# One quarter of a weight load, issued as sixteen pieces of eight partitions

## The chip, the cores and the metric

One core of a Trainium2 chip runs the kernel. The metric is the device time of one execution in microseconds (us); the time before is the median of three runs. The profile is one execution more, recorded by the hardware profiler, and it has its own time. The core's compute engines are PE (matrix multiply, its results go to PSUM), DVE (elementwise and reductions), ACT (activation functions) and POOL. SP (SyncE) computes nothing: it issues the transfers, in program order, and 16 DMA engines carry them between HBM and SBUF, the on-chip memory of 128 partitions.

## The reference, cut to what matters

Four requests decode one token each: attention of 32 heads over a cache of 4096 keys and values, an output projection `wo`, then a dense block with a mish activation. Weights and caches are bfloat16.

```python
x = A_x                                                   # [4, 1, 640]
q = (layernorm(x) @ wq) as [b, h, 1, 128]
scores = einsum("bhqd,bhkd->bhqk", q, k_cache) * 128**-0.5    # k_cache [4, 32, 4096, 128]
o = einsum("bhqk,bhkd->bhqd", softmax(scores), v_cache)
h = x + o as [4, 1, 4096] @ wo                            # wo [4096, 640]
hh = layernorm(h) @ w1 + b1                               # w1 [640, 1728]
out = h + (hh * tanh(softplus(hh))) @ w2                  # w2 [1728, 640]
```

K and V are 134 MB each; all weights together are 15 MB.

## The kernel before

The work goes in 32 steps g (`NG`), each with four heads of one request: g = 4 * hq + b, hq a group of four heads, b the request. One step needs one K tile and one V tile, each [128 partitions, 128 rows, 128], 32 KB a partition and 4.19 MB in all. A partition holds 128 keys of one head, so a tile is one transfer with 128 long contiguous rows (`load_kv`, issue on L91). Both pools have two buffers (`KBUFS`, `VBUFS`); only the last K and V tiles come in two halves.

In step g, DVE multiplies the K tile by the broadcast query (L297), PE adds up the products with identity matmuls in PSUM (L304), DVE finishes the sums (L316), and PE, DVE and ACT make the softmax one step later (L329 to L347). PE multiplies the V tile of step g-1 by the softmax weights (`pv`, L231).

The order of the issues on SP is written out by hand in the loop: after the products of step g comes the K load of step g+2 (L374), then `pv(g - 1)`, then the V load of step g+1 (L383). The K load waits until the K buffer is free, that is until DVE and PE are done with K of step g; the V load waits until PE is done with V of step g-1.

`wo` (4096 x 640, 5.24 MB) comes into the buffer that `wq` used, `wo_sb`, in four quarters of `WOC` = 8 heads, at steps 8 to 11 (`WO_AT`), each right behind that step's V load. A quarter is one transfer: `(h p) n -> p h n` puts row h*128+p into partition p, so each partition gets eight runs of 640 elements, 1280 bytes each, 1024 runs in all. Behind the first quarter goes `b1` as a single row. Its first readers: `project(hq)` (L274) multiplies four heads of `wo_sb` with the normalised attention; groups 0 to 3 run at steps 14 to 17, group 6 at step 30 and group 7 after the loop (`PROJ_AT`), and the last quarter holds the heads of groups 6 and 7.

The dense block's weights follow behind the last V tile: w1 in one transfer into a freed K buffer (L421), w2 in five (L422 to L425).

A framework adds the semaphores from the program's reads and writes. Each DMA signals on one of eight completion semaphores, which it takes in turn over all DMAs of the program (`DMAHW0` to `DMAHW7` in the built program). A DMA that takes a semaphore is held, on SP, until the transfer that had it before has landed, unless SP has seen that already.

Of the kernel before, what the change touches and what calls it, by code (L numbers as in the profile page):

```python
# [16 lines left out]
def kernel(  # L17
# [21 lines left out]
    nc = tc.nc  # L39

    B, Sq, D = A_x.shape
    _, H, Sk, Dh = A_k_cache.shape
# [14 lines left out]
    WOC = 8  # L57
# [36 lines left out]
    def load_k(g):  # L94
        return load_kv(kpool, "kt", A_k_cache, g)

    def load_v(g):
        return load_kv(vpool, "vt", A_v_cache, g)
# [35 lines left out]
    for q in range(G):  # L134
        nc.vector.tensor_copy(
            out=sel[:, :, q, q * PH : (q + 1) * PH],
            in_=ident[0:N, 0:N].unsqueeze(2).to_broadcast([N, N, PH]),
# [45 lines left out]
    def q_chunk(n):  # L183
        q_ps = ps.tile([N, QC], FP32, tag="qq")
        for c in range(DC):
            nc.tensor.matmul(  # L186
                q_ps[:, :],
                lhsT=xT[:, c, :],
                rhs=wq_sb[:, c, n * QC : (n + 1) * QC],
                start=(c == 0),  # L190
                stop=(c == DC - 1),
            )
        nc.scalar.copy(out=q_all[:, n * QC : (n + 1) * QC], in_=q_ps[:, :])  # L193
# [31 lines left out]
    def pv(g):  # L225
        hq, b = divmod(g, N)
        vt = vts.pop(g)
        if b == 0:
            ot[hq] = ps.tile([128, N, G], FP32, tag="ot", bufs=2, name=f"ot{hq}")
        for r in range(R):  # L230
            nc.tensor.matmul(  # L231
                ot[hq][:, b, :],
                lhsT=vt[:, r, :],
                rhs=e2[g % NE2][:, r, :],
                start=(r == 0),
                stop=(r == R - 1),
            )
# [3 lines left out]
    def row_sums(hq):  # L241
        l_ps = ps.tile([128, N, G], FP32, tag="small")
        nc.tensor.matmul(  # L243
            l_ps[:, :, :],
            lhsT=ones_f[:, :],
            rhs=rs2[:, hq * N : (hq + 1) * N, :],
            start=True,
            stop=True,
        )
        rls[hq] = work.tile([128, N, G], FP32, tag="rl", name=f"rl{hq}")  # L250
        nc.vector.reciprocal(out=rls[hq][:, :, :], in_=l_ps[:, :, :])  # L251

    def normalise(hq):
        nc.vector.tensor_tensor(
            out=otn[:, hq, :, :],
            in0=ot.pop(hq)[:, :, :],
            in1=rls.pop(hq)[:, :, :],
            op=ALU.mult,
        )
# [12 lines left out]
    wo_sb = []  # L272

    def project(hq):  # L274

        for h in range(hq * G, (hq + 1) * G):
            for c in range(DC):
                nc.tensor.matmul(  # L278
                    yT[:, c, :],
                    lhsT=wo_sb[0][:, h, c * 128 : (c + 1) * 128],  # L280
                    rhs=otn[:, hq, :, h % G],
                    start=(h == 0 and c == 0),
                    stop=(h == H - 1 and c == DC - 1),
                )
# [3 lines left out]
    def mul_and_sum(g, part):  # L288

        hq, b = divmod(g, N)  # L290
        r0 = part * RP
        kt = kts[g][:, r0 : r0 + RP, :]
        s_ps = ps.tile([128, RP, W], FP32, tag="s", bufs=2, name=f"s{g}_{part}")
        s_of[g, part] = s_ps
        for k in range(NQ):
            d0 = k * DQ
            nc.vector.tensor_tensor(  # L297
                out=kt[:, :, d0 : d0 + DQ],
                in0=kt[:, :, d0 : d0 + DQ],
                in1=qbs[:, hq, b, d0 : d0 + DQ].unsqueeze(1).to_broadcast([128, RP, DQ]),  # L300
                op=ALU.mult,
            )
            for d in range(d0, d0 + DQ, W):
                nc.tensor.matmul(  # L304
                    s_ps[:, :, :],
                    lhsT=ident[:, :],
                    rhs=kt[:, :, d : d + W],
                    start=(d == 0),
                    stop=(d == Dh - W),
                )  # L310
            yield

    def finish_sum(g, part):
        if part == 0:
            s_sbs[g] = work.tile([128, R], FP32, tag="s_sb", name=f"s_sb{g}")
        nc.vector.tensor_reduce(  # L316
            out=s_sbs[g][:, part * RP : (part + 1) * RP],
            in_=s_of.pop((g, part))[:, :, :],
            axis=AX.X,
            op=ALU.add,  # L320
        )

    def softmax(g):

        s_sb = s_sbs.pop(g)
        pm = work.tile([128, 1], FP32, tag="pm", name=f"pm{g}")
        nc.vector.tensor_reduce(out=pm[:, :], in_=s_sb[:, :], axis=AX.X, op=ALU.max)  # L327
        tr_ps = ps.tile([128, 128 + G], FP32, tag="tr", name=f"tr{g}")
        nc.tensor.matmul(  # L329
            tr_ps[0:1, 0:128], lhsT=pm[:, :], rhs=ident_f[:, :], start=True, stop=True  # L330
        )
        yield
        mx = work.tile([1, G], FP32, tag="mx", name=f"mx{g}")
        nc.vector.tensor_reduce(  # L334
            out=mx[:, :],
            in_=tr_ps[0:1, 0:128].rearrange("o (a b) -> o a b", a=G),
            axis=AX.X,
            op=ALU.max,
        )

        nb_ps = tr_ps[:, 128 : 128 + G]
        nc.tensor.matmul(nb_ps, lhsT=nscale[:, :], rhs=mx[:, :], start=True, stop=True)  # L342
        nb = work.tile([128, G], FP32, tag="nbs", name=f"nbs{g}")
        nc.scalar.copy(out=nb[:, :], in_=nb_ps)  # L344
        for q in range(G):
            p0, p1 = q * PH, (q + 1) * PH
            nc.scalar.activation(  # L347
                out=e2[g % NE2][p0:p1, :, q],
                in_=s_sb[p0:p1, :],
                func=ACT.Exp,  # L350
                bias=nb[p0:p1, q : q + 1],
                scale=SCALE,
                accum_out=rs2[p0:p1, g, q : q + 1],
            )
        yield

    for g in range(NG):
        hq, b = divmod(g, N)
        for part in range(NP):
            now = mul_and_sum(g, part)  # L360
            before = None
            next(now)
            if part > 0:
                finish_sum(g, part - 1)
            elif g >= 1:
                finish_sum(g - 1, NP - 1)
                before = softmax(g - 1)
                next(before)
            next(now)
            if before is not None:  # L370
                next(before)
        kts.pop(g)
        if g + 2 < NG:
            kts[g + 2] = load_k(g + 2)  # L374
        if 1 <= g < NG - 1:
            pv(g - 1)
            if b == 0:
                row_sums(hq - 1)
                normalise(hq - 1)
        if g in PROJ_AT:  # L380
            project(PROJ_AT[g])
        if g + 1 < NG:
            vts[g + 1] = load_v(g + 1)  # L383
        for n in Q_AT.get(g, ()):
            q_chunk(n)
            q_broadcast(n)
        if g in WO_AT:

            if not wo_sb:
                wo_sb.append(wbig.tile([128, H, D], BF16, tag="w", name="wo_sb"))  # L390
            h0 = WO_AT[g] * WOC
            nc.sync.dma_start(
                out=wo_sb[0][:, h0 : h0 + WOC, :],
                in_=A_wo.rearrange("(h p) n -> p h n", p=128)[:, h0 : h0 + WOC, :],
            )
            if WO_AT[g] == 0:
                nc.sync.dma_start(out=b1_row[:, :], in_=B_b1.rearrange("(o f) -> o f", o=1))
        if g == B1_AT:
            b_ps = ps.tile([128, FC], FP32, tag="small", name="b_ps")
            for c in range(FC):  # L400
                cols, fw = f_chunk(b1_row[:, :], c)
                nc.tensor.matmul(
                    b_ps[0:fw, c : c + 1],
                    lhsT=cols,
                    rhs=ident[0:1, 0:1],
                    start=True,
                    stop=True,
                )
            nc.vector.tensor_copy(out=b1T[:, 0:C2], in_=b_ps[:, 0:C2])
            nc.vector.tensor_copy(out=b1T[0:FREM, C2:FC], in_=b_ps[0:FREM, C2:FC])  # L410
# [44 lines left out]
    for dst in (h2T, hc):  # L455
        nc.vector.tensor_tensor(
            out=dst[:, :, :],
# [11 lines left out]
    for c in range(FC):  # L469
# [9 lines left out]
        if c == 4:  # L479
# [3 lines left out]
                out=std[:, :], in_=v_ps[:, :], func=ACT.Sqrt, bias=eps_t[:, :], scale=1.0  # L483
# [5 lines left out]
        out=h1n[:, :, :],  # L489
# [6 lines left out]
        out=h1s[:, :, :],  # L496
# [9 lines left out]
        out=tb[:, :, :],  # L506
# [8 lines left out]
        out=ta[:, :, :], in0=tb[:, :, :], scalar1=-0.5, scalar2=-1.0, op0=ALU.mult, op1=ALU.add  # L515
# [4 lines left out]
        out=act_t[:, :, :],  # L520
# [10 lines left out]
    for i, (w2, c) in enumerate(w2_of):  # L531
# [11 lines left out]
        out=oT[:, :, :].rearrange("p n c -> p c n"),  # L543
# [46 lines left out]
```

## Time and profile before

| | |
|---|---|
| median of 3 runs | 678.72 us (678.62 to 679.22) |
| the profiled execution | 679.1 us, span from first to last instruction 677.2 us |
| busy PE, DVE, ACT | 467.1, 352.9, 95.1 us |
| read from HBM | 283.35 MB, 418 GB/s over the span |
| chain that ended last, K loads / w loads | 61% / 4% of the span |
| the four `wo` issues | 1280 KB each, 30.7 us (median) from issue to landing |
| K and V issues | 31 + 31 of 4096 KB, 2 + 2 of 2048 KB |

How to read it: a row of the profile names the line, the engine and the tiles (out<-in); `xcount` is how many instructions it stands for. SPq rows are issues: their duration is how long SP was held by the issue, not how long the transfer took. The slices are 40 equal parts of the span; a digit is the busy share in tenths. The chain follows the work that ended last back to what released it at each step.

### The profile page before, as it was taken

The page shows a single profiled execution, that of the slowest core. Times are in us where ns is not written, and L with a number is a line of the kernel's source. Part 1 is how long each engine was busy: PE and PEld are TensorE (multiplying, and loading weights), DVE is VectorE, ACT ScalarE, POOL GpSimd, SP SyncE. Part 2 cuts the span into 40 slices and gives each one's busy share as a digit, 9 for nine tenths or more (in the row PEclk, how much of TensorE's full clock was granted, in tenths as well). Part 3 has the DMA queues.
Part 4 walks back from the last instruction along what each step waited for, and adds up shares of the span by engine and source line. Part 5 has one row for each costly group of instructions (what it writes and reads, how often), then busy time and mean ns, then how long its engine had stood idle before and what let it go on. Part 6 is the DMA issues. An engine that isn't in the chain of part 4 may idle for free.

```text
span 677.2 us, 12413 instructions
## 1 busy us (share of the span) xinstructions
PE 467.1 (69%) x5761; PEld 258.3 (38%) x5761; DVE 352.9 (52%) x304; ACT 95.1 (14%) x313; POOL 2.4 (0%) x13
## 2 busy tenths in 40 slices
PE   1588898787676475467677668767666776666965
PEld 0234445444333341343344434323333432333444
DVE  2476445456655356336654545665454566645722
ACT  0022112212101111011100111110011111101131
POOL 1000000000000000000000000000000000000000
PEclk9997678987667786687676788876788876767875
DMA  9999999999999999999999999999999999999993
GB/s 376 434 433 429 433 430 432 432 431 430 430 431 416 429 417 411 429 423 429 433 431 428 426 431 431 429 429 433 432 429 431 429 433 433 429 426 425 431 407 144
DMA packets 15211, 284.15 MB, mean 420 GB/s; under 512 B 1267, under 2 KB 5559, under 8 KB 6584
## 3 DMA queue, kind: packets, MB, share of 16 engines
q1 hardware_dynamic: 15152, 283.36, 98.2%
q8 instruction: 45, 0.74, 0.4%
q14 instruction: 6, 0.05, 0.0%
q10 hardware_dynamic: 8, 0.01, 0.0%
HBM read 283.35 MB, written 0.01 MB: 418 GB/s over the span
## 4 chain that ended last, share of the span: by engine, by line
DMA 66%; PE 16%; DVE 16%; issue 1%; ACT 0%; SPq 0%; DVEq 0%
DMA kt<-in_A_k_cache_dram 61%; PE s L304 14%; DVE kt L297 14%; DMA w<-in_B_w_dram 4%; DVE s_sb L316 2%; PE tr L329 1%; DVE mx L334 0%; PE h_ps L472 0%; PE y2T L534 0%; PE ot L231 0%; PE q_ps L186 0%; PE qb_ps L200 0%; ACT q_all L193 0%; DVE tb L517 0%; PE var_ps L449 0%
## 5 line engine op out<-in xcount | busy, mean ns | idle before, releaser
L304 PE MATMUL s<-kt,ident 128*128 128x512 bf16 x1024 | 299.5, 446 | 175.0 <-DVE kt L297 174.8
L297 DVE TENSOR_TENSOR kt<-kt,qbs 128x4096 bf16<-128x4096 bf16 x128 | 291.5, 2279 | 219.0 <-DMA kt<-in_A_k_cache_dram 219.0
L304 PEld LDWEIGHTS <-ident 128*128 128x128 bf16 x1024 | 107.8, 109 | 326.3 <-issue 178.4
L231 PEld LDWEIGHTS <-vt 128*128 128x128 bf16 x4096 | 109.0, 96 | 11.3 <-DMA vt<-in_A_v_cache_dram 2.2
L231 PE MATMUL ot<-e,vt 128*128 128x4 bf16 x4096 | 109.0, 165 | 4.0 <-DMA vt<-in_A_v_cache_dram 2.1
L347 ACT ACTIVATE e<-s_sb,nbs 32x128 bf16<-32x128 f32 x128 | 74.0, 578 | 2.5
L344 ACT COPY nbs<-tr 128x4 f32<-128x4 f32 x32 | 5.2, 162 | 467.3 <-PE tr L342 467.3
L316 DVE TENSOR_REDUCE s_sb<-s 128x64 f32<-128x512 f32 x64 | 43.5, 680 | 3.6 <-PE s L304 3.6
L347 ACT ACTIVATION_READ_ACCUMULATOR e<-s_sb,nbs 32x1 f32 x128 | 32.2, 252 | 0.0
L251 DVE RECIPROCAL rl<-l_ps 128x16 f32<-128x16 f32 x8 | 2.1, 257 | 45.3 <-PE l_ps L243 45.3
L334 DVE TENSOR_REDUCE mx<-tr 1x4 f32<-1x128 f32 x32 | 8.9, 279 | 30.5 <-PE tr L329 30.5
L186 PE MATMUL q_ps<-wq_sb,xT 128*4 128x512 bf16 x40 | 14.7, 517 | 9.2 <-DMA wq_sb<-in_A_wq_dram 9.2
L200 PE MATMUL qb_ps<-q_all,sel 4*128 4x128 bf16 x128 | 13.6, 286 | 5.3 <-ACT q_all L193 5.3
L329 PE MATMUL tr<-ident_f,pm 128*1 128x128 f32 x64 | 16.0, 344 | 1.2 <-DVE pm L327 1.2
L200 PEld LDWEIGHTS <-sel 4*128 4x128 bf16 x128 | 12.3, 128 | 10.7 <-issue 10.7
L193 ACT CAST q_all<-q_ps 4x512 bf16<-4x512 f32 x8 | 4.6, 574 | 74.6 <-PE q_ps L186 74.6
L342 PEld LDWEIGHTS tr<-mx,nscale 1*128 1x128 f32 x64 | 9.4, 183 | 13.8 <-issue 11.5
L329 PEld LDWEIGHTS tr<-ident_f,pm 128*1 128x1 f32 x64 | 2.8, 81 | 26.0 <-issue 26.0
L342 PE MATMUL tr<-mx,nscale 1*128 1x4 f32 x64 | 12.2, 258 | 0.4 <-DVE mx L334 0.4
L327 DVE TENSOR_REDUCE pm<-s_sb 128x1 f32<-128x128 f32 x32 | 9.2, 286 | 1.1
L186 PEld LDWEIGHTS <-xT 128*4 128x4 bf16 x40 | 3.4, 97 | 15.1 <-issue 13.5
L278 PE MATMUL yT<-otn,wo_sb 128*128 128x4 bf16 x160 | 5.5, 165 | 1.9 <-issue 1.6
(74 smaller groups left out, 51.1 us busy)
## 6 DMA issues: line engine op xcount, KB each, us to landing
kt<-in_A_k_cache_dram SPq DMA_DIRECT2D x31, 4096.0 KB, 25.7
vt<-in_A_v_cache_dram SPq DMA_DIRECT2D x31, 4096.0 KB, 32.0
wq_sb<-in_A_wq_dram SPq DMA_DIRECT2D x1, 5120.0 KB, 14.9
wo_sb<-in_A_wo_dram SPq DMA_DIRECT2D x4, 1280.0 KB, 30.7
kt<-in_A_k_cache_dram SPq DMA_DIRECT2D x2, 2048.0 KB, 23.1
vt<-in_A_v_cache_dram SPq DMA_DIRECT2D x2, 2048.0 KB
w<-in_B_w_dram SPq DMA_DIRECT2D x1, 2160.0 KB, 28.4
w<-in_B_w_dram SPq DMA_DIRECT2D x3, 640.0 KB, 19.9
```

The source lines that it names most:

```text
L186: nc.tensor.matmul(q_ps[:, :], lhsT=xT[:, c, :], rhs=wq_sb[:, c, n * QC : (n + 1) * QC], start=(c == 0), stop=(c == DC - 1),)
L200: nc.tensor.matmul(qb_ps[:, b * Dh : (b + 1) * Dh], lhsT=sel[:, b, q, :], rhs=q_all[:, h * Dh : (h + 1) * Dh], start=(q == 0), stop=(q == ...
L231: nc.tensor.matmul(ot[hq][:, b, :], lhsT=vt[:, r, :], rhs=e2[g % NE2][:, r, :], start=(r == 0), stop=(r == R - 1),)
L278: nc.tensor.matmul(yT[:, c, :], lhsT=wo_sb[0][:, h, c * 128 : (c + 1) * 128], rhs=otn[:, hq, :, h % G], start=(h == 0 and c == 0), stop=(h ...
L297: nc.vector.tensor_tensor(out=kt[:, :, d0 : d0 + DQ], in0=kt[:, :, d0 : d0 + DQ], in1=qbs[:, hq, b, d0 : d0 + DQ].unsqueeze(1).to_broadcas ...
L304: nc.tensor.matmul(s_ps[:, :, :], lhsT=ident[:, :], rhs=kt[:, :, d : d + W], start=(d == 0), stop=(d == Dh - W),)
L316: nc.vector.tensor_reduce(out=s_sbs[g][:, part * RP : (part + 1) * RP], in_=s_of.pop((g, part))[:, :, :], axis=AX.X, op=ALU.add,)
L327: nc.vector.tensor_reduce(out=pm[:, :], in_=s_sb[:, :], axis=AX.X, op=ALU.max)
L329: nc.tensor.matmul(tr_ps[0:1, 0:128], lhsT=pm[:, :], rhs=ident_f[:, :], start=True, stop=True)
L334: nc.vector.tensor_reduce(out=mx[:, :], in_=tr_ps[0:1, 0:128].rearrange("o (a b) -> o a b", a=G), axis=AX.X, op=ALU.max,)
L342: nc.tensor.matmul(nb_ps, lhsT=nscale[:, :], rhs=mx[:, :], start=True, stop=True)
L347: nc.scalar.activation(out=e2[g % NE2][p0:p1, :, q], in_=s_sb[p0:p1, :], func=ACT.Exp, bias=nb[p0:p1, q : q + 1], scale=SCALE, accum_out=r ...
```

## The change

The issue of a `wo` quarter becomes a loop over the partitions. For the first three quarters it runs once, over all 128. For the last quarter (`h0 + WOC == H`, step 11) it runs sixteen times, over eight partitions each; a piece is 8 partitions x 8 runs of 1280 bytes, 80 KB. The sixteen pieces write what the one transfer wrote, on the same queue and at the same place in the program: behind V of step 12, ahead of K of step 14.

```diff
@@ -389,10 +389,15 @@
             h0 = WO_AT[g] * WOC
-            nc.sync.dma_start(
-                out=wo_sb[0][:, h0 : h0 + WOC, :],
-                in_=A_wo.rearrange("(h p) n -> p h n", p=128)[:, h0 : h0 + WOC, :],
-            )
+
+            pp = 8 if h0 + WOC == H else 128
+            for p0 in range(0, 128, pp):
+                nc.sync.dma_start(
+                    out=wo_sb[0][p0 : p0 + pp, h0 : h0 + WOC, :],
+                    in_=A_wo.rearrange("(h p) n -> p h n", p=128)[
+                        p0 : p0 + pp, h0 : h0 + WOC, :
+                    ],
+                )
             if WO_AT[g] == 0:
```

The pieces take sixteen turns of the eight completion semaphores where the one transfer took one. Every DMA behind them takes another of the eight than before.

## The prediction

> **What bounds the kernel now.** I read the page first: the DMA rows of the slices, the queues, the chain.
>
> ```profile
> DMA  9999999999999999999999999999999999999993
> GB/s 376 434 433 429 433 430 432 432 431 430 430 431 416 429 417 411 429 423 429 433 431 428 426 431 431 429 429 433 432 429 431 429 433 433 429 426 425 431 407 144
> ...
> q8 instruction: 45, 0.74, 0.4%
> ...
> q10 hardware_dynamic: 8, 0.01, 0.0%
> ...
> DMA 66%; PE 16%; DVE 16%; issue 1%; ACT 0%; SPq 0%; DVEq 0%
> ...
> x_bf<-in_A_x_dram ACTq DMA_DIRECT2D x1, 5.0 KB
> ```
>
> The 16 DMA engines are full in 39 of 40 slices at about 432 GB/s, 27 GB/s each. DVE and PE sit on the chain only between two K loads. So time is what the engines must carry, plus any stretch in which they have nothing queued. The q10 row is for later: a load of 4 rows left 8 packets, four with data and four that close it.
>
> Second, the end of the run by windows (last two columns: share of the 16 engines, GB/s).
>
> ```profile
> 656.00:662.00 6.00, 3.67 (x118) 3.58 (x118) 0.26 (x1) 0.00 (x0) 0.00 (x0) 0.50 0.99 379
> 662.00:668.00 6.00, 3.45 (x81) 3.19 (x79) 1.20 (x8) 0.00 (x0) 0.00 (x0) 0.50 0.56 218
> 668.00:672.00 4.00, 1.90 (x51) 1.90 (x51) 1.74 (x7) 2.00 (x4) 0.00 (x0) 0.50 0.29 118
> ```
>
> The share falls to about half at 662 us and the rest runs on to 671: half of the engines are done nine microseconds early. The packet records say which: the 45 instruction fetches (q8, 16 KB) go round eight engines only, and each puts its engine back by 1.6 us. I call these the later eight, the others the earlier eight. At vt12 (the V load of step 12) the earlier eight close at 287.4 to 288.7 us, the later eight at 290.6 to 292.4.
>
> Third, SyncE's own line of time around the last quarter of wo (start, duration).
>
> ```profile
> 249.53 11.22 SPq L91 DMA_DIRECT2D kt<-in_A_k_cache_dram  x1
> 260.86 4.90 SPq L91 DMA_DIRECT2D vt<-in_A_v_cache_dram  x1
> 265.81 0.43 SPq L392 DMA_DIRECT2D wo_sb<-in_A_wo_dram  x1
> 272.67 11.27 SPq L91 DMA_DIRECT2D kt<-in_A_k_cache_dram  x1
> 284.04 6.12 SPq L91 DMA_DIRECT2D vt<-in_A_v_cache_dram  x1
> ```
>
> These are kt13, vt12, the last quarter, kt14 and vt13. kt14 is handed over at 272.67 and lands 33.6 us later, at 306.2: it stands more than 20 us deep in the queue, which is why the engines never run dry.
>
> Fourth, the chain in order of time (start, length).
>
> ```profile
> 249.53 33.56 DMA kt<-in_A_k_cache_dram
> ```
> ```profile
> 638.29 28.37 DMA w<-in_B_w_dram
> ```
>
> kt13 lands at 283.1. The end hangs on w1, which the later eight bring at 666.7; a delay of the later eight in the middle thus reaches the end whole.
>
> **The change, part by part.** *Computation.* No compute instruction is added or moved, and the bytes are the same. The quarter is first read by the projection of step 30, some 300 us later, so its own landing may slip at no cost.
>
> *Who carries the bytes.* A store of 20 rows at the end shows how a short transfer is spread:
>
> ```profile
> DMA packets 30, 0.01 MB, mean 2 GB/s; under 512 B 30, under 2 KB 30, under 8 KB 30
> ...
> out_dram<-out_bf SPq DMA_DIRECT2D x1, 5.0 KB
> ```
>
> 30 packets are 20 rows and 10 closings, so ten engines of two rows; the 4-row load used four. Eight rows then go to eight engines, one each. Followed packet by packet, b1's single row and two of the four rows of x sit on engines of the earlier eight, so I put the pieces there. [...] Today each engine carries 64 packets of 1280 B; vt11 lands at 268.7 and the third quarter behind it at 272.3 (242.88 + 29.4), so a quarter takes 3.5 us. After the change the earlier eight carry 128 packets, 7.1 us, and the later eight none: -3.5 us on the eight that set the end.
>
> *SyncE's waits.* This is where I see the cost. In the built program each DMA takes one of eight completion semaphores in turn and waits until the last transfer on that semaphore has landed. One wo DMA used up one turn; sixteen go round twice. Pieces 0 to 3 go at once (265.8 to 267.5). Piece 4 waits for vt11 (268.7), piece 5 for the third quarter (272.3), piece 6 for kt13 (283.1), piece 7 for vt12. vt12 has no landing row; the quarter behind it landed at 265.81 + 30.7 = 296.5, less 3.5 gives 293.0. kt14 and vt13 stand behind these on SyncE, and kt13 and vt12 were the last large loads in the queue. So the cover of 20 us is used up, and the later eight go idle when vt12 is through.
>
> *Restart.* From 293.0 SyncE issues pieces 7 to 15 and then kt14. An issue cost 0.33 us (plain K load) to 0.58 (the first V load); I take the wo row, 0.43, since it is the same kind: 9 x 0.43 = 3.9, so kt14 goes at 296.9 (295.9 to 298.2). Piece 15 waits for piece 7, kt14 for piece 8; both have long landed. From issue to first data the store of the result took 0.8 us; wq, on empty queues, landed 14.9 us after its issue, where 5.24 MB at 432 GB/s are 12.1, so 2.8 more with its landing. kt14 is a large load like wq: 296.9 + 2.8 + 9.7 (4.19 MB at 432) = 309.4, against 306.2: +3.2 for the last engine. With the bounds, low 295.9 + 0.8 + 9.7 = 306.4 and high 298.2 + 2.8 + 9.7 = 310.7: +0.2 to +4.5.
>
> *Stagger.* Most of the later eight closed vt12 at 290.6, not at 292.4. The restart lines all of them up, and those that were early still have the next fetches before them, 1.6 us each. They lose 298.5 - 290.6 = 7.9 and save 3.5: +4.4. The one that was last loses about 2.7 but gets a fetch fewer. At the end the group was within 2.2 us, so I add 1.3 to the 3.2 (bounds 0 and 1.6). **Sum: +4.5 us, between +0.2 and +6.1.** The earlier eight end their pieces near 298.3 (nine pieces of 0.47 from 294) and lose 7 us of their lead of 9, which is hidden.
>
> Made against the profiled execution's own 679.1 us (span 677.2 and 1.9 around it): 683.6. The median of the runs is 0.4 below that execution, so I predict 683.2.
>
> **The rivals.** *Neighbouring partitions share a way into SBUF.* If four engines that write four adjacent partitions had the 27 GB/s of one engine between them, a piece would take 4 x 10,240 B / 27 = 1.5 us instead of 0.47. Nine pieces from 294 would last until 307.6, and the earlier eight would start kt14 16 us late; their lead of 9 is gone and about 8 us reach the end: 686.7. If the first seven collide fully too, all sixteen take 24 us from 288, to 312: 691. For: one engine never shows more than 27 GB/s. Against: two rows of x, both in partitions 0 to 3, were written in the same 70 ns at 53 ns each; but 2.5 KB are little. [...]
>
> *The relief wins.* Without the pause the later eight are 3.5 us lighter: 675.2, faster. It decides if kt14 is with the engines before vt12 ends on the later eight, so issued by about 289.8. For: half the engines do idle for nine microseconds at the end. Against: piece 7's wait for vt12 ends only at 293.0.
>
> *No difference.* If small pieces cost SyncE 0.1 us and data follows 0.8 us after the issue, kt14 starts at 294.7; from 290.6 that is 4.1 idle less 3.5 saved: 679.3. No issue row is below 0.32.
>
> *The pieces sit on the later eight* (the change relieves the wrong ones): seven follow vt12 until 294, nine more until 298.4, then kt14: the same 683. It changes the reason, not the number.
>
> **How the numbers follow.** Forecast 0.52 (with the pieces on either eight, 680 to 685); sharing 0.34, some of it above 691; relief 0.06; no difference 0.05; a larger loss of another kind 0.03. A change of 0.2%, 1.4 us, is about what a measurement can tell. Faster 0.06, same 0.06, slower 0.88. The range 680.3 to 691 leaves out the relief, the no-difference case, and the full collision.
>
> **What would show it.** Right: SyncE's line has seven pieces by 283.6 and nine from about 293 to 297 with kt14 behind; the DMA share falls to a half or less between 293 and 298; kt14 lands near 309; the share at the end falls later and more steeply than at 662. Sharing: pieces of 1 us and more, and an end where the early half is gone. Wrong: kt14 issued before 290, or no gap.

## The result and the profile after

The changed kernel takes 688.32 us (median of five runs, 687.45 to 690.62) against 678.79 (678.62 to 679.22) for the kernel before: a ratio of 1.0148, 95% interval 1.0127 to 1.0169, or +9.5 us. The profiled execution is the slowest of the five, 690.6 us with a span of 688.8, so it stands 11.6 us above the span of 677.2 before. The trace is read by the 11.6, the medians by the 9.5.

The page's slices of the changed kernel, and its chain by engine:

```profile
DMA  9999999999999999969999999999999999999994
GB/s 379 441 427 425 430 427 436 432 425 433 427 431 417 430 421 413 352 175 428 434 433 435 423 427 429 435 429 429 433 426 433 431 425 435 427 436 424 432 404 170
...
DMA 67%; PE 17%; DVE 15%; issue 1%; SPq 0%; ACT 0%; DVEq 0%
```

Two slices of 17.2 us fall, to 352 and 175 GB/s (276 to 310 us). All others are as full as before. A stretch that moves 432 GB/s when full has lost (2 - (352 + 175) / 432) x 17.2 = 13.4 us there; some 2 us come back at the end of the run. The SyncE line of time around that hole (start, duration):

```profile
260.65 4.90 SPq L91 DMA_DIRECT2D vt<-in_A_v_cache_dram  x1
265.60 36.20 SPq L395 DMA_DIRECT2D wo_sb<-in_A_wo_dram  x16
302.81 0.35 SPq L91 DMA_DIRECT2D kt<-in_A_k_cache_dram  x1
303.56 0.35 SPq L91 DMA_DIRECT2D vt<-in_A_v_cache_dram  x1
```

vt12, then the sixteen pieces, then kt14, which is handed over at 302.81 instead of 272.67. SyncE's waits between 255 and 310 us (total us, times, longest) say for what:

```profile
SPq L395 <- DMA vt<-in_A_v_cache_dram: 13.2, 2, 12.1
SPq L395 <- DMA kt<-in_A_k_cache_dram: 10.8, 1, 10.8
SPq L395 <- DMA wo_sb<-in_A_wo_dram: 6.9, 9, 3.3
```

Two waits for V tiles, one for a K tile, nine for wo: the third quarter (3.3) and, for each of the last eight pieces, the piece eight turns earlier. Those eight take 3.6 us together. The chain in order of time (start, length) joins it to the end:

```profile
265.60 30.65 DMA wo_sb<-in_A_wo_dram
...
296.27 6.45 DMA wo_sb<-in_A_wo_dram
...
302.81 14.96 DMA kt<-in_A_k_cache_dram
```

kt14 lands at 317.8. Before, it landed at 306.2; the difference, 11.6 us, is the whole of what the span grew by. Nothing else in the run is needed to account for it.

What the engines did in the hole, by windows of 2 us (last two columns: share of the 16 engines, GB/s):

```profile
286.00:288.00 2.00, 2.00 (x6) 0.70 (x5) 1.97 (x3) 0.00 (x0) 0.00 (x0) 0.50 1.03 378
288.00:290.00 2.00, 2.00 (x10) 0.74 (x9) 1.53 (x3) 0.00 (x0) 0.00 (x0) 0.94 0.84 191
290.00:292.00 2.00, 1.57 (x9) 0.77 (x7) 2.00 (x2) 0.70 (x3) 0.00 (x0) 1.00 0.87 218
292.00:294.00 2.00, 1.54 (x8) 0.58 (x6) 2.00 (x2) 1.78 (x8) 0.00 (x0) 1.00 0.31 75
294.00:296.00 2.00, 1.54 (x8) 0.72 (x8) 0.40 (x1) 0.00 (x0) 0.00 (x0) 1.00 0.11 36
300.00:302.00 2.00, 0.17 (x4) 0.09 (x1) 0.23 (x2) 0.00 (x0) 0.00 (x0) 0.98 0.56 96
304.00:306.00 2.00, 0.00 (x0) 0.00 (x0) 0.00 (x0) 0.00 (x0) 0.00 (x0) 0.50 0.92 206
```

There are two kinds of loss. From 292 to 296 the share is 0.31 and 0.11: the engines have nothing to do, because SyncE is waiting. From 288 to 292 and from 304 to 306 they are 0.84 to 0.92 busy and still move about 200 GB/s, half of what the same share moves elsewhere: the packets themselves are long. The packet records give it: a 1280-byte packet of the first three quarters took 55 to 60 ns, one of these pieces mostly 100 to 124 (medians by microsecond, 288 to 290 and 298 to 305); the 32 KB packets of K and V beside them took 1.4 to 2.6 us, elsewhere 1.21. Not all of this is collision: the first packets of a K load into empty engines are long anyway (1.4 to 2.2 us in the kernel with almost no bytes in its pieces, below), so for kt14's first ones only what goes beyond that counts.

### The profile page after: what moved, and what is told of

It is laid out like the page before. It is cut to its first block, busy times and chain, and to the rows that moved or that the text cites. A ratio compares the mean times of both kernels' runs of the same rounds, so it can differ in the third digit from the quotient of the medians.

```text
span 688.8 us, 12429 instructions
## 1 busy us (share of the span) xinstructions
PE 467.2 (68%) x5761; PEld 258.2 (37%) x5761; DVE 353.0 (51%) x304; ACT 95.1 (14%) x313; POOL 2.4 (0%) x13
## 2 busy tenths in 40 slices
DMA packets 15323, 284.15 MB, mean 413 GB/s; under 512 B 1379, under 2 KB 5671, under 8 KB 6696
## 4 chain that ended last, share of the span: by engine, by line
DMA 67%; PE 17%; DVE 15%; issue 1%; SPq 0%; ACT 0%; DVEq 0%
DMA kt<-in_A_k_cache_dram 57%; PE s L304 14%; DVE kt L297 13%; DMA wo_sb<-in_A_wo_dram 5%; DMA w<-in_B_w_dram 4%; DVE s_sb L316 1%; PE tr L329 1%; PE ot L231 0%; DVE mx L334 0%; PE h_ps L477 0%; PE y2T L539 0%; SPq L91 0%; DVE tb L522 0%; PE var_ps L454 0%; SPq L104 0%
## 5 line engine op out<-in xcount | busy, mean ns | idle before, releaser
L186 PE MATMUL q_ps<-wq_sb,xT 128*4 128x512 bf16 x40 | 13.2, 473 | 9.1 <-DMA wq_sb<-in_A_wq_dram 9.1
L342 PEld LDWEIGHTS tr<-mx,nscale 1*128 1x128 f32 x64 | 9.4, 182 | 13.8 <-issue 10.6
```

The source lines that it names most:

```text
L186: nc.tensor.matmul(q_ps[:, :], lhsT=xT[:, c, :], rhs=wq_sb[:, c, n * QC : (n + 1) * QC], start=(c == 0), stop=(c == DC - 1),)
```

## The experiments

The theory after the result: the waits are as forecast, and the rest comes from engines that write into partitions which another engine is writing. The rivals: the reading side is what collides; the waits alone make it all; the neighbourhood of the eight partitions matters, not who else writes there. Times are medians; the kernel before, run beside each group of them, took 678.8 to 679.1 us. In the edits `wo_v` is `wo` as `p h n`.

**Partitions four apart.** Same number of pieces, same place, same waits; a piece takes every fourth partition of 32.

```diff
-            for p0 in range(0, 128, pp):
+            parts = [slice(b + r, b + 32, 4) for b in range(0, 128, 32) for r in range(4)]
+            for s in parts:
```

> The sixteen pieces keep their eight partitions, their number, their place and their semaphore waits, but a piece takes partitions four apart instead of neighbours, and reads rows four apart. If neighbours share a way into SBUF (S), the 1280-byte packets go back from about 106 ns to 55 to 60, no K or V packet in 287 to 306 us is stretched, K of step 14 is issued near 297 and lands near 309, and the time is about 683. If the waits on SyncE alone make the loss (W), nothing changes: 688. If reading eight neighbouring rows from HBM is what slows (M): also about 683.

Measured 685.70 us, ratio 1.0101 (1.0086 to 1.0116): faster than the change by 2.6. The packets are back at a median of 55 ns and vt12 lands at 292.9, but there is a new cost, in SyncE's line of time and in the issues by line (ns, min/median/max):

```profile
265.67 33.67 SPq L399 DMA_DIRECT2D wo_sb<-in_A_wo_dram  x16
299.46 0.37 SPq L91 DMA_DIRECT2D kt<-in_A_k_cache_dram  x1
```
```profile
L399 SPq DMA_DIRECT2D wo_sb<-in_A_wo_dram x16: 677/677/829, 265.7 to 298.7; - x16
```

A strided piece holds SyncE 0.68 us; in the changed kernel the median is 0.27. So kt14 goes at 299.46, still 2.6 us after the forecast of 296.9, and its last engine is through at 312.4. The collision is gone, and the dearer issue takes its place: nine issues cost 9 x (0.68 - 0.27) = 3.7 us more.

**Which side collides.** Pieces write eight neighbours as in the change, and read rows four apart.

```diff
+            for j, s in enumerate(parts):
+                nc.sync.dma_start(out=wo_sb[0][j * pp : (j + 1) * pp, h0 : h0 + WOC, :],
+                                  in_=wo_v[s, h0 : h0 + WOC, :])
```

> The pieces write eight neighbouring partitions as in the change, but read rows of wo four apart; the rows of the last quarter so stand in a permuted order and the output is not the reference's. S: 688, packets near 106 ns as in the change. M (the reading side): about 683, packets 55 to 60 ns. Together with the run of partitions four apart this tells the writing from the reading side.

688.16 us, 1.0139 (1.0124 to 1.0154); the packets' medians by microsecond are 95 to 114 ns (288 to 291 and 297 to 301) and up to 166 behind that. The time is no different from the change, so the rows that are read don't matter: the collision is on the side that writes.

**The waits with almost no bytes.** Seven heads of the quarter go in one transfer over 128 partitions, the eighth in sixteen pieces of 10 KB.

```diff
+            h1 = h0 + WOC - (h0 + WOC == H)
+            nc.sync.dma_start(out=wo_sb[0][:, h0:h1, :], in_=wo_v[:, h0:h1, :])
+            if h1 < h0 + WOC:
+                for p0 in range(0, 128, 8):
+                    nc.sync.dma_start(out=wo_sb[0][p0 : p0 + 8, h1 : h1 + 1, :],
+                                      in_=wo_v[p0 : p0 + 8, h1 : h1 + 1, :])
```

> Seven of the last quarter's eight heads come in one transfer of 128 partitions, only the eighth in sixteen pieces of eight partitions: the same waits on SyncE, an eighth of the bytes in pieces. W: SyncE is held until V of step 12 has landed at about 293, ten issues follow, K of step 14 lands near 309, and the time is 682 to 684. If the waits cost nothing and only the pieces' bytes do (S alone): 678.8 to 680.

685.27 us, 1.0094 (1.0077 to 1.0111). SyncE's line, and the windows of the pause:

```profile
266.04 33.09 SPq L398 DMA_DIRECT2D wo_sb<-in_A_wo_dram  x16
299.25 0.35 SPq L91 DMA_DIRECT2D kt<-in_A_k_cache_dram  x1
```
```profile
292.00:294.00 2.00, 1.87 (x8) 0.77 (x8) 2.00 (x2) 1.95 (x8) 0.00 (x0) 1.00 0.50 172
294.00:296.00 2.00, 1.21 (x6) 0.58 (x6) 0.73 (x1) 0.17 (x2) 0.00 (x0) 1.00 0.08 28
296.00:298.00 2.00, 2.00 (x64) 1.69 (x61) 0.00 (x0) 0.00 (x0) 0.00 (x0) 1.00 0.07 15
298.00:300.00 2.00, 2.00 (x80) 1.99 (x77) 0.00 (x0) 0.00 (x0) 0.00 (x0) 0.83 0.16 39
```

Here the engines are almost empty for six microseconds, and until 299 no K or V packet is longer than 1.32 us: the waits of this kernel cost +6.4 without any collision. That is 1.3 above the range expected, since one more landing stands in the way: a piece waits for the seven-head transfer, which is through at 296.1, 3.0 us behind vt12. So +6.4 is not the price of the waits in the change. Without the extra 3.0 it would be about +3.4, and the kernel with partitions four apart, less the 3.7 of its dearer issue, gives 6.9 - 3.7 = +3.2 (both estimates). The change's own waits are then worth about 3 of its 9.5 us. From kt14's issue (299.25) to its last engine (311.6) it is 12.4 us, the 12.5 that the forecast gave a restart.

**No waits.** Two pieces in each of steps 11 to 18, behind the V load, so that SyncE never stands: once with eight neighbours, once four apart, once sixteen apart, and once as eight pieces of sixteen neighbours, one a step. The quarter's own transfer at step 11 is left out; of the edits the first is shown in its main lines, and of the other three only the line that picks the partitions.

```diff
+        if HQ + 3 <= g < HQ + 11:
+            for p0 in range((g - HQ - 3) * 16, (g - HQ - 2) * 16, 8):
+                nc.sync.dma_start(out=wo_sb[0][p0 : p0 + 8, H - WOC : H, :],
+                                  in_=wo_v[p0 : p0 + 8, H - WOC : H, :])
```
```diff
+            parts = [slice(b + r, b + 32, 4) for b in range(0, 128, 32) for r in range(4)]   # four apart
+            parts = [slice(r, 128, 16) for r in range(16)]                                   # sixteen apart
+            parts = [slice(b, b + 16) for b in range(0, 128, 16)]                            # sixteen neighbours
```

> The sixteen pieces of neighbouring partitions go two to a step, behind the V load of steps 11 to 18, so no issue waits for a load that is still deep in the queue. If the engines that carry the pieces are all of the eight that end early (as my prediction had it), the later eight are 3.5 us lighter and the time is 675 to 676.5, with S hidden in the early eight's lead. If some of them are among the eight that set the end, these carry 3.6 us more, with sharing up to 8 us more: 681 to 687. W alone says 679 or less.

> The pieces go two to a step as in the spread run, but take partitions four apart. If neighbouring partitions are what stretches the K and V packets (S), all K and V packets stay at 1.21 us and the 21 us of the spread run are gone: what is left is who carries the pieces (R). In the change and in the spread run the closings of a piece come six with the early engines and two with the late ones; those two then carry 64 packets of 1280 bytes more than before, 3.6 us: 680 to 683. If all eight were early ones: 675 to 676.5. If any small transfer between large ones costs 1.3 us a piece whatever its partitions: about 700.

> Two pieces a step, partitions sixteen apart over all 128. If adjacency is what counts, this is as good as four apart. [...]

> Eight pieces of sixteen neighbouring partitions, one to a step: sixteen engines with one row each, so every engine carries as many packets as before the change. R is out of play and SyncE waits for nothing. S: four neighbours still share a way, and a piece costs about what one of eight neighbours cost in the spread run, 1.3 us or up to twice that: 689 to 700. If only the eight-engine split costs: 679.

| pieces | us | ratio (interval) |
|---|---|---|
| eight neighbours | 700.00 | 1.0315 (1.0299 to 1.0330) |
| four apart | 690.66 | 1.0173 (1.0159 to 1.0187) |
| sixteen apart | 701.25 | 1.0328 (1.0314 to 1.0342) |
| sixteen neighbours | 694.50 | 1.0228 (1.0214 to 1.0242) |

All are slower than before, three of them clearly slower than the change itself, although no issue of a piece waits for a landing any more: the collision is far dearer beside running loads than in a pause. Of the four forecasts only the one for sixteen neighbours held. Eight neighbours came above every case that was expected (687 at most), four apart between two of them (683 and 700), and sixteen apart stands 10.6 us above four apart, where adjacency alone would have made the two the same. Neighbours as such are not the point, since sixteen apart is as bad. The GB/s lines of the pages with eight neighbours and with four apart tell where to look:

```profile
GB/s 387 424 435 433 424 436 428 428 425 435 429 433 418 412 430 418 383 393 424 395 384 378 396 399 380 380 429 421 429 432 424 432 433 420 435 432 421 392 403 71
```
```profile
GB/s 379 440 425 429 430 431 428 428 431 429 435 427 413 430 417 423 423 433 425 425 435 375 389 411 371 373 429 427 433 426 433 427 431 429 429 430 422 420 399 112
```

With neighbours the slices of the eight steps are low, 378 to 399 but for one of 424 (from slice 17 on, 279 us). Four apart, the first four steps, whose pieces go to partitions 0 to 63, run at 423 to 435, as if nothing were there; the low slices begin where partitions 64 to 127 do. Their windows show 288 GB/s at a full share (368 to 372 us) against 431 (288 to 292). The K and V packets say the same: from 280 to 361 us 99 in 100 take at most 1.27 us, from there to 440 one in ten takes 1.78 us or more.

**Pieces of six partitions.** Six engines carry a piece instead of eight, by the count of packets: 15,323, or 112 more than before, as twenty pieces with six closings and two with four give, less the sixteen of the one transfer. Two pieces go in a step, from step 11 on. The bases go in steps of 24, where the kernel with partitions four apart, whose first four steps ran at 423 to 435 GB/s, has 32.

```diff
+            parts = [slice(b + r, b + 24, 4) for b in range(0, 120, 24) for r in range(4)]
+            parts += [slice(120 + r, 128, 2) for r in range(2)]
```

> Pieces of six partitions four apart (twenty of them, and two of four for the last eight partitions), two to a step over steps 11 to 21: six engines should carry them instead of eight. If the first six engines are the six early ones, the ten others are 3.5 us lighter and nothing else is added: 675 to 676.5, below the kernel before. If the two late ones are among the first six: 680 to 684, as with eight.

698.42 us, 1.0289 (1.0275 to 1.0303). The number of engines is not the point either, and that miss gave the theory its present form: each engine has partitions of its own in the big loads (its home), and a piece costs no more than its bytes where every engine writes at home. No record names the partitions that an engine writes, so the theory is tried by times.

**Home and off by one engine.** The quarter is whole again, as before the change; eight extra pieces, two a step in steps 14 to 17, load the rows of 32 of its partitions again, each row twice (0.66 MB more). They start at partition 0 or at partition 4 (each kernel has one of the two `s` lines); nothing else differs.

```diff
+        if HQ + 6 <= g < HQ + 10:
+            for r in (0, 1) if g % 2 == 0 else (2, 3):
+                s = slice(0 + r, 0 + r + 32, 4)          # home
+                s = slice(4 + r, 4 + r + 32, 4)          # one engine off
+                nc.sync.dma_start(out=wo_sb[0][s, H - WOC : H, :], in_=wo_v[s, H - WOC : H, :])
```

> The kernel before, and beside it eight pieces of eight partitions four apart, two to a step in steps 14 to 17, that load rows of partitions 0 to 31 of the last quarter a second time (each row twice in all): 655 KB more. Theory H (home): a DMA engine that writes the partitions it also writes in the large K and V loads collides with nobody, and the first of eight engines has partitions 0 to 3, the next 4 to 7 and so on. Here every engine writes its own: K and V packets stay at 1.21 us, and the time is that of 64 more packets on eight engines, two of them late ones: 679 to 682.5. Theory N (any small transfer beside the large ones costs 0.7 to 1.4 us): 685 to 690.

> As the run before, but the eight pieces begin at partition 4: the same number of engines, packets and bytes, still partitions four apart, only that each engine now writes the four partitions of its neighbour. H: every piece collides with the K and V packets of another engine; packets of 1.5 to 2 us return, and the time is 8 x 1.4 = 11 us above the kernel before: 688 to 692. If it were adjacency within a piece (S as first put), nothing collides: 679 to 682.5.

682.17 us, 1.0041 (1.0027 to 1.0054), against 691.06, 1.0182 (1.0168 to 1.0196). The same bytes, number, stride and place, moved by four partitions, cost 8.9 us more, and both times are as expected. The slices of the home kernel, then of the other:

```profile
GB/s 381 433 430 432 429 428 427 429 432 432 428 430 414 431 414 418 420 425 430 430 429 426 428 429 430 430 432 430 430 427 432 430 430 430 430 429 422 430 399 109
```
```profile
GB/s 385 434 429 425 432 435 426 432 425 433 431 429 416 429 419 419 410 433 428 430 406 397 389 419 374 435 427 429 425 434 431 431 429 427 429 428 427 410 400 92
```

Slices 21 to 25 fall to 374 to 419 in the second alone. The +3.3 of the home kernel can be plain work: eight engines carry 8 x 10,240 B = 82 KB more each, 3.0 us at 27 GB/s (an estimate, with 432 / 16 for one engine). By the home theory the first kernel's pieces are at home and the second's each one engine off. Measured is the 8.9 us between the two; which engine wrote which partitions was not shown.

**Half at home.** The change's place and waits; the eight pieces of partitions 0 to 63 four apart, the others eight neighbours as in the change.

```diff
+                parts = [slice(b + r, b + 32, 4) for b in (0, 32) for r in range(4)]
+                parts += [slice(b, b + 8) for b in range(64, 128, 8)]
```

> The change with the same place and waits, but the first eight pieces take partitions four apart in 0 to 63 (every engine its own), the other eight neighbours in 64 to 127. H: the seven that run beside V of step 12 stretch nothing, it lands at 293.0, and the eight neighbours run when no K or V load is in the queue; K of step 14 is issued near 297.3 and lands near 310: 683 to 685, below the change (688) and below sixteen pieces four apart (685.7), which held SyncE 0.7 us an issue. If H is wrong and half the pieces keep half the loss: 686 to 688.

690.39 us (686.39 to 691.03), 1.0157 (1.0136 to 1.0179), so no better than the change, and the expected gain is missed. The first half of it came true: vt12 lands at 293.1, and kt14 is issued 0.5 us behind the 297.3 expected:

```profile
265.69 31.09 SPq L400 DMA_DIRECT2D wo_sb<-in_A_wo_dram  x16
297.77 0.36 SPq L91 DMA_DIRECT2D kt<-in_A_k_cache_dram  x1
```

It then takes 20.9 us to land. The neighbour pieces are still under way, and its packets that start before 304 take 3.5 to 4.9 us. The windows after it:

```profile
298.00:302.00 4.00, 2.98 (x107) 2.85 (x103) 0.23 (x2) 0.00 (x0) 0.00 (x0) 0.82 1.09 125
302.00:306.00 4.00, 0.00 (x0) 0.00 (x0) 0.00 (x0) 0.00 (x0) 0.00 (x0) 0.50 1.16 112
```

All engines count as busy at 112 to 125 GB/s, and a piece closes on its eight engines within 0.5 us, every 1.3 to 1.8 us (medians 297.5, 298.8, 300.1, 301.7, 303.4, 305.2, 306.9, 308.4). A piece is 81,920 B; at the mean of 1.56 us its eight engines get 53 GB/s in all (46 to 63 in single intervals), about what two engines move elsewhere (2 x 27). In the change the eight engines were up to 7 us apart in time (piece 0 closed between 289.3 and 296.3), and its last nine pieces were issued 0.8 us apart on the mean. Whether pieces lose less where their engines are out of step wasn't tried by itself, and the closings don't settle it: for the last eight pieces seven of the engines were within 0.6 to 1.4 us of each other again, and closed one every 0.9 to 1.0 us. Also kt14, which runs beside the pieces from 298 on in the half-at-home kernel and from 303 on in the change, is another difference.

## Why the prediction was wrong

The direction held, and 688.3 lies inside the range, but the loss is twice the 4.5 forecast. By its own steps:

- **SyncE's waits: right.** Seven pieces went by 283.23, piece 7 when vt12 had landed, kt14 behind piece 15, and the engines ran dry. The kernel with almost no bytes in its pieces pays +6.4 for such waits alone, 3.0 of it for a landing that the change doesn't wait for; the change's own waits come out at about +3.3 (the estimate above), close to the +3.2 that the sum had for waits and restart together. The four kernels without such waits show none of the hole: behind the first slice and ahead of the last they move at least 366 GB/s in every slice, where the changed kernel falls to 175.
- **Restart: the step that failed.** It put kt14 at 296.9 = 293.0 + 9 x 0.43 and its landing at 309.4. Measured: 302.81 and 317.8. Three terms carry the 8.4 us. vt12, whose packets were stretched by the first seven pieces, landed at 295.6 (+2.6). The nine pieces took 7.2 us instead of 3.9 (+3.3): the issue is cheaper than thought, 0.27, but from piece 8 on each waits for the piece eight turns before (piece 8 goes at 296.27, piece 0 closed at 296.3). The forecast had called those "long landed". And kt14 needed 15.0 us instead of 12.5 (+2.5), as one engine had pieces until 308.3 and kt14's eight packets behind them (8 x 1.21 = 9.7). The forecast gave the pieces 0.47 us each, on engines with a lead of 9 us, so that nothing of them reached vt12 or kt14. Where the pieces don't collide, vt12 lands at 292.9 and kt14 needs 12.9 us from its issue (partitions four apart).
- **Stagger: not found in the change.** It added 1.3 for the later eight; kt14's slip of 11.6 is the whole slip of the span. (A part of it shows where nothing collides: in the kernel with almost no bytes in its pieces kt14 slips by 5.4 us and the span grows by 6.3, with partitions four apart by 6.2 and 6.7.) The 298.5 in its working, when kt14's data would start, is derived nowhere; 296.9 and the 0.8 to first data give 297.7. So 8.4 - 1.3 = 7.1 is what the sum lacked in the profiled execution, 5.1 in the medians.
- **Who carries the bytes: half right.** Eight rows do go to eight engines (112 packets more than before, 15,323: 128 closings where the one transfer had 16), but not to the earlier eight. In the half-at-home kernel piece 0 closes six times at 288.3 to 289.5 and twice at 291.6, as the early and the late engines close vt12 (287.9 to 289.1 and 291.2 to 293.1): two of the eight are late ones. The home kernel says the same by its time: work on engines with a lead of 9 us would have cost nothing, and it cost 3.3. That all sixteen pieces share one set of eight engines stands in no record; the +3.3 of the home kernel agrees with it for its eight pieces, at 3.0 estimated. So the relief of 3.5 could not come: two engines that set the end got heavier. That also corrects the rival "the relief wins", which hung on a matter of timing only.
- **The sharing rival: right in kind, not in its condition.** It gave 686.7 and named partitions next to each other. (Its own terms, 16 us late less a lead of 9, make 7 at the end and not 8, so 685.7.) That four neighbours have one engine's rate between them is its own supposition and no run shows it; the half-at-home kernel shows 53 GB/s for eight. The pair at home and one engine off (682.17 and 691.06) has partitions four apart in both, so adjacency doesn't decide there. By the home theory it is whether an engine writes where another one is writing: in the change from 288 to 292 that can be vt12's engines as well as the piece's own neighbours, later the neighbours and kt14's. Its price of 1.5 us a piece is met in the half-at-home kernel, while in the change the last nine pieces were issued 0.8 us apart (7.2 / 9); why they cost less there stays open. What it weighed against itself, two rows of x written in 70 ns without loss, was 2.5 KB in an empty queue.
- **What would show it.** The gap, the nine late pieces and an end that falls later and more steeply than at 662 were all there. kt14's landing near 309 was not, and the signs named for sharing came only in part: the last pieces closed on seven of their eight engines every 0.9 to 1.0 us, where 1 and more was named, and the early half still ends ahead of the other. The end stands in these windows of the changed kernel:

```profile
668.00:674.00 6.00, 2.87 (x107) 2.78 (x105) 0.00 (x0) 0.00 (x0) 0.00 (x0) 0.50 1.00 382
674.00:680.00 6.00, 3.27 (x75) 3.03 (x73) 1.19 (x8) 0.27 (x2) 0.00 (x0) 0.50 0.74 282
680.00:684.00 4.00, 1.90 (x52) 1.87 (x51) 1.74 (x7) 1.72 (x3) 0.00 (x0) 0.50 0.19 78
```

The share is 1.00 until 674; before, it was 0.56 from 662.

None of the versions beat the kernel before. The nearest, the home kernel at 682.2, carries bytes that it doesn't need.

**What stays open.** Beside running loads, 32 KB packets that start at the time of a piece are stretched on nearly all engines (eight neighbours, 287 to 289 us: 1.6 to 2.1 us each), where the home theory would have it only on those whose homes are written. In the half-at-home kernel, too, the eight packets of kt14 that start near 299 are all stretched alike, to 3.5 to 4.3 us. The runs don't show why. Which two of the eight engines are late ones was counted, not identified. And the split of the +9.5 is an estimate: about 3 for the waits, the other 6 for the collision and for the waits that it lengthens. No kernel had the change's waits alone; the two without collision, +6.4 and +6.9, each pay about 3 for something of their own.

## What to carry to other kernels

A large load split into small ones is priced by the completion semaphores that it uses up: with eight in turn, the piece that meets a load still deep in the queue stops the issuing engine, and all that is queued behind it, until that load has landed (here up to 12.1 us for one load, and kt14 went 30.1 us later than before). A piece over few partitions is carried by few engines (eight closings for eight rows here), and which partitions it writes beside running loads can cost more than its bytes (8.9 us for eight pieces moved by four partitions); split along the free dimension instead, so that each piece still covers all 128 partitions (the one seven-head transfer here did, and K and V packets stayed at 1.21 to 1.32 us; several such pieces weren't tried). If a kernel is bound by transfers, look for slices in which the engines are busy and the GB/s are low: here that came with stretched packets (shares of 0.84 to 0.92 at 191 to 218 GB/s), while a low share was a wait (0.31 and 0.11).

## What was not expected of the hardware

- Pieces moved by four partitions, from 0 to 4, beside running loads: 8.9 us for eight of 80 KB, 1.1 us each. The others agree once the doubled load of the late engines, 3.5 us, is taken off (an estimate): eight neighbours (21.2 - 3.5) / 16 = 1.1, sixteen apart (22.2 - 3.5) / 16 = 1.2, four apart (11.6 - 3.5) / 8 = 1.0 for the eight pieces above partition 63. Sixteen neighbours, with sixteen closings a piece (15,323 packets), 15.4 / 8 = 1.9 for twice the bytes.
- Eight engines writing eight neighbouring partitions got about 53 GB/s in all where they closed within 0.5 us of each other: 1.3 to 1.8 us for a piece of 80 KB (half at home, with kt14 beside it from 298 on).
- An issue over eight partitions four apart holds SyncE for 0.68 us, sixteen apart for about 0.6, over eight neighbours for 0.27 to 0.33.
